# The first layer of three of eight experts as seven block products in place of eight, its stages set between second-layer tiles

## The chip, the cores and the metric

The kernel runs on one core of a Trainium2 chip. The time is that of the device from start to end of one execution, in microseconds. The engines are TensorE (PE, with PEld for its weight loads), VectorE (DVE), ScalarE (ACT), GpSimd (POOL) and SyncE (SP, which only issues DMAs here). Each works through a list of instructions of its own, in order, and waits for others by semaphores.

## The reference

A filter along the sequence in the frequency domain, then a mixture of eight experts, each of which takes exactly 2,496 tokens. Tokens are given out greedily by the sorted logits.

```python
def _attn_ref(x, filt_r, filt_i):              # x (8, 2496, 256)
    X = np.fft.rfft(x, axis=1)
    F = (filt_r + 1j * filt_i)[None, :, :]
    y = np.fft.irfft(X * F, n=x.shape[1], axis=1)

def _moe_ref(x, w_gate, w1, w2):               # x (19968, 256), E = 8
    cap = N // E
    logits = x @ w_gate
    order = np.argsort(-logits.flatten())
    ...
    for e in range(E):
        mask = assigned == e
        h = np.maximum(x[mask] @ w1[e], 0.0)   # 256 -> 1024
        out[mask] = h @ w2[e]                  # 1024 -> 256
```

## The kernel before

Up to 448 us the filter runs as matmuls with cosine tables. The logits `lg` are made beside it. From there to the end the eight experts e0 to e7 follow one another on PE, and this is the part that the change touches.

**One expert.** `Ffn.run` takes its tokens in five groups: four of 512 and one of 448. fp32 precision is kept by splitting each operand into a high part (rounded to fp32r, by ACT) and a low part (the rest, by DVE), and three products: high x high, high x low, low x high. `gather` brings tokens by indirect DMA, `turn` transposes them on PE (L837, four transposes for 256 tokens) and splits them (L840 on ACT, L841 on DVE). `first(g, f)` makes one of eight chunks of 128 hidden features for a group: two halves of the 256 inputs x three products, six matmuls of 512 (448) columns into one PSUM tile `pz` of four (L859). ACT writes the relu's high part (L865), DVE the low part (L873; L876 in the last group), for some chunks POOL (L868, L869). The second layer goes by tiles of 128 tokens: for each of the eight chunks a matmul of 512 columns (L913, the high part by both halves of the weights) and one of 256 (L914). ACT copies the result (L923), POOL adds its halves (L924) and scatters it (L925). The last tile has 64 tokens and takes 16 matmuls of 256 columns (L909). The weights of an expert are loaded whole (L804, on POOL) and split in pieces of 512 columns (L816 on ACT, L817 on DVE).

**What sets the order.** On PE the program's order holds. In group g the first layer of group g+1 is laid between the second-layer tiles of g (`firsts(g + 1, ORD[t])`). The lists of DVE, ACT and POOL come from a scheduler at build time and are fixed then.

**The routing.** While experts run, the next expert's tokens are chosen: `threshold` searches a limit by counting matmuls (L567, L580) with DVE work between them (L559, L577, L597 to L619), then come exact selection, a correction of the logits by `pen` (L696 on DVE, eight operations L727 on ACT) and the places of the tokens (L756 to L773). Each `yield c` of the expert's program passes c microseconds to `Pump.feed`, whose clock decides between which matmuls the next routing step stands. The routing of phase 7, the last, runs beside e5.

Of the kernel before, what the change touches and what calls it, by code (L numbers as in the profile page):

```python
# [27 lines left out]
NP, NZ, MZ, NXO, ZB, NH = 5, 4, 8, 4, 2, 10  # L28
# [441 lines left out]
class Route:  # L470
# [10 lines left out]
    def setup(s):  # L481
# [35 lines left out]
        s.tmp = t("tmp", [117, S, 8])  # L517
        s.iota, s.sidx = t("iota", [117, 512], F16), t("sidx", [128, 20])
        io = s.tmp.rearrange("p s e -> p (s e)")[:, :512]
# [117 lines left out]
    def phase(s, ph):  # L637
# [23 lines left out]
        vc, need, tot, mem = v("vc", [128, 1]), v("need", [128, 1]), v("tot", [117, 4]), v("m0", [117, S])  # L661
# [7 lines left out]
        if ph < 7:  # L669
# [15 lines left out]
            ga, eqm, cum = v("ga", [117, S]), v("eqm", [117, S]), v("cum", [117, S])  # L685
# [42 lines left out]
        with s.tc.issue_after(s.last):  # L728
            t, t3 = v("u", [117, S]), v("u2", [117, S])
# [54 lines left out]
class Ffn:  # L784


    def __init__(s, tc, i, xs, out, cp, ww, zp, ps):
# [6 lines left out]
        s.wt, s.xg, s.xT = {}, {}, {}  # L794

    def weights(s, e, widx):
# [3 lines left out]
        hl = [[s.ww.tile([128, 2048], F32R, name=f"w0{h}", bufs=2) for h in 'hl']]  # L800
        s.w2b = s.ww.tile([128, 2, 2048], F32R, name="w1", bufs=2)
        hl.append([s.w2b[:, k] for k in range(2)])
        s.wt[e] = (raw, hl, s.w2b)
        s.load = lambda k: nc.gpsimd.indirect_dma_start(out=raw[k], out_offset=None, in_=(s.w1, s.w2)[k], in_offset=off).ins  # L804

    def split(s, e, part):

        nc = s.nc
        raw, hl, _ = s.wt[e]
        k, h = divmod(part, 4)  # L810
        src, (hi, lo) = raw[k], hl[k]
        if k == 0:
            h, j = divmod(h, 2)
            h += 2 * j
        src, hi, lo = (t[:, 512*h:512*h+512] for t in (src, hi, lo))
        nc.scalar.copy(hi, src)  # L816
        nc.vector.tensor_tensor(lo, src, hi.bitcast(F32), op=OP.subtract)  # L817

    def gather(s, e, g, ids):
        for t in range(4*g, 4*g + 4):  # L820
            n = min(128, CAP - 128*t)
            xg = s.xg[e, t] = s.wp.tile([128, D], F32, name="xg", bufs=8)
            s.lastg = s.nc.gpsimd.indirect_dma_start(out=xg[:n], out_offset=None, in_=s.xs,  # L823
# [18 lines left out]

    def run(s, e, pump, hook):

        nc = s.nc
        ids = pump.out[e]
        out_rows = s.out
        _, ((w1h, w1l), (w2h, w2l)), w2 = s.wt[e]
        hs = {}

        def first(g, f):
# [4 lines left out]
            for k in range(2):  # L856
                sl = slice(1024*k+128*f, 1024*k+128*f+128)
                for w, x in ((w1h, xh), (w1h, xl), (w1l, xh)):
                    nc.tensor.matmul(p[:, :n], w[:, sl], x[:, k, :n], start=m == 0, stop=m == 5)  # L859
                    m += 1  # L860
                yield 0.65 * n / 512
# [283 lines left out]
```

## Time and profile before

| what | us |
|---|---|
| median of three runs | 1456.03 (1455.15 to 1462.08) |
| the profiled execution | 1465.58 |
| its span | 1463.8 |
| e5, e6, e7 begin | 1109.88, 1229.63, 1345.79 |
| last matmul ends | 1458.95 |
| PE busy | 1391.3 (95% of the span) |
| DVE, ACT, POOL busy | 955.6, 723.7, 663.6 |

The profiled execution lies above the median of the runs without a profile; all stretches below are its own. A matmul's record is longer than its distance to the next one, since matmuls overlap in the pipeline. So lengths of a stream are read from starts. A row of waits names the waiting instruction, then what released it.

### The profile page before, as it was taken

The numbers are of one execution on the slowest core, as the hardware profiler recorded it, in microseconds if no ns is written. First come the engines' busy times: TensorE is split into PE (matmuls) and PEld (weight loads), VectorE is DVE, ScalarE is ACT, GpSimd is POOL, SyncE is SP. The second block draws the span as 40 slices with busy tenths as digits, with TensorE's granted clock in tenths as the row PEclk, the third lists the DMA queues.
The fourth block names the chain that finished last, engine by engine and source line by source line (L and its number), as shares of the span: only waits on it lengthen the run. The fifth ranks groups of instructions, "written<-read, shape, count | busy, mean of one in ns | idle before, by whom it ended". The sixth has DMA issues, their size and how long they took to land. (4 is left out here: it accounts for less than half of the span.)

```text
span 1463.8 us, 24844 instructions
## 1 busy us (share of the span) xinstructions
PE 1391.3 (95%) x9127; PEld 1148.7 (78%) x9127; DVE 955.6 (65%) x2574; ACT 723.7 (49%) x1686; POOL 663.6 (45%) x729
## 2 busy tenths in 40 slices
PE   7899999998997999899999899999999999999998
PEld 6889899776445787677778788787878888888887
DVE  5666676576566789666876976977877854432231
ACT  5666677534473345344544533644553654533332
POOL 5433344243004745553664546366545644445423
PEclk9999999999998999999999999999999999999999
DMA  8554454888892102112110211211211221111100
GB/s 263 185 148 143 126 163 116 237 239 206 328 348 74 51 22 95 53 35 75 59 52 25 98 49 39 90 51 48 95 37 50 102 95 52 38 48 46 42 26 27
DMA packets 54780, 149.17 MB, mean 102 GB/s; under 512 B 9258, under 2 KB 29866, under 8 KB 50706
## 3 DMA queue, kind: packets, MB, share of 16 engines
q0 software_dynamic: 17552, 57.72, 12.1%
q1 hardware_dynamic: 9803, 47.11, 10.6%
q10 hardware_dynamic: 27304, 42.76, 9.5%
q8 instruction: 72, 1.18, 0.3%
q14 instruction: 49, 0.40, 0.1%
HBM read 83.89 MB, written 63.70 MB: 101 GB/s over the span
## 5 line engine op out<-in xcount | busy, mean ns | idle before, releaser
L913 PE MATMUL py<-w,hl 128*128 128x512 f32 x1216 | 445.6, 405 | 0.5 <-ACT hl L865 0.3
L914 PE MATMUL py<-w,hl 128*128 128x256 f32 x1216 | 341.9, 281 | 1.0 <-DVE hl L873 0.6
L865 ACT ACTIVATE hl<-pz 128x512 fp32r<-128x512 f32 (+1 forms) x320 | 186.8, 586 | 214.7 <-PE pz L859 189.0
L859 PE MATMUL pz<-xo,w0h 128*128 128x512 f32 (+1 forms) x640 | 264.4, 413 | 10.3 <-DVE hl L876 3.7
L913 PEld LDWEIGHTS py<-w,hl 128*128 128x128 f32 x1216 | 229.8, 189 | 51.4 <-issue 1.2
L924 POOL TENSOR_TENSOR y<-y 128x256 f32<-128x256 f32 x152 | 122.4, 806 | 311.2 <-ACT y L923 309.9
L859 PE MATMUL pz<-xo,w0l 128*128 128x512 f32 (+1 forms) x640 | 249.9, 390 | 0.0
L859 PE MATMUL pz<-z,w0h 128*128 128x512 f32 (+1 forms) x640 | 249.3, 390 | 0.2 <-issue 0.2
L914 PEld LDWEIGHTS py<-w,hl 128*128 128x128 f32 x1216 | 230.7, 190 | 5.3 <-DVE hl L873 2.2
L873 DVE SCALAR_TENSOR_TENSOR hl<-pz,hl 128x512 fp32r<-128x512 f32 x227 | 155.0, 687 | 116.0 <-ACT hl L865 101.8
L823 POOL DMA_INDIRECT xg<-xs,xid x160 | 168.3, 1052 | 135.8 <-issue 41.0
L923 ACT COPY y<-py 128x512 f32<-128x512 f32 x152 | 89.1, 586 | 282.8 <-PE py L914 188.5
L925 POOL DMA_INDIRECT out<-y,oid x160 | 174.5, 1090 | 48.1 <-POOL y L924 33.6
L859 PEld LDWEIGHTS pz<-xo,w0h 128*128 128x128 f32 x640 | 122.0, 191 | 33.7 <-DVE hl L873 3.8
L232 POOL TENSOR_TENSOR P<-P 128x256 f32<-128x256 f32 x80 | 58.9, 737 | 184.6 <-DVE P L230 184.5
L859 PEld LDWEIGHTS pz<-xo,w0l 128*128 128x128 f32 x640 | 121.3, 190 | 24.1
L859 PEld LDWEIGHTS pz<-z,w0h 128*128 128x128 f32 x640 | 122.0, 191 | 17.3 <-DVE z L841 1.0
L216 ACT COPY Y<-p 64x240 f32<-64x240 f32 (+1 forms) x304 | 116.0, 382 | 30.4 <-PE p L209 19.8
L209 PE MATMUL p<-cS,xr 117*128 117x120 f32 x688 | 100.5, 283 | 7.2 <-DMA xr<-xl 7.1
L559 DVE TENSOR_TENSOR Gm<-M,thr 117x1232 bf16<-117x1232 f32 (+2 forms) x80 | 105.5, 1329 | 0.2
L209 PEld LDWEIGHTS p<-cS,xr 117*128 117x128 f32 x688 | 91.0, 199 | 11.2 <-issue 4.7
L224 PE MATMUL p<-cW,Y 128*128 128x128 f32 x640 | 88.7, 281 | 2.3 <-ACT Y L216 1.5
(229 smaller groups left out, 2274.2 us busy)
## 6 DMA issues: line engine op xcount, KB each, us to landing
zd<-zt ACTq DMA_DIRECT2D x80, 256.0 KB
z<-zd SPq DMA_DIRECT2D x18, 600.0 KB
xs<-xo ACTq DMA_DIRECT2D x18, 600.0 KB
xr<-xl SPq DMA_DIRECT2D x6, 1404.0 KB
xr<-xl SPq DMA_DIRECT2D x7, 1111.5 KB
xr<-zd SPq DMA_DIRECT2D x8, 600.0 KB
xs<-xr ACTq DMA_DIRECT2D x8, 600.0 KB
xs<-Y ACTq DMA_DIRECT2D x6, 600.0 KB
```

Of the source, the lines that this page charges most:

```text
L209: nc.tensor.matmul(p[:, q-q0, :120], s.xr[b][:, q], s.cS1, start=True, stop=True)
L216: x = (nc.vector.tensor_copy if dve else nc.scalar.copy)(dst, src)
L559: nc.vector.tensor_tensor(Gm[:, s0:s1, :m], s.M[:, s0:s1].unsqueeze(2).to_broadcast([117, s1 - s0, m]), thr[:117].unsqueeze(1).to_broadcas ...
L823: s.lastg = s.nc.gpsimd.indirect_dma_start(out=xg[:n], out_offset=None, in_=s.xs, in_offset=bass.IndirectOffsetOnAxis(ap=ids[0][:n, t:t+1] ...
L859: nc.tensor.matmul(p[:, :n], w[:, sl], x[:, k, :n], start=m == 0, stop=m == 5)
L865: s.lasta = nc.scalar.activation(h[:, :n], p[:, :n], AF.Relu).ins
L873: nc.vector.scalar_tensor_tensor(l[:, :n], p[:, :n], 0.0, h[:, :n].bitcast(F32), op0=OP.max, op1=OP.subtract)
L913: nc.tensor.matmul(pp, hs[g][f][:, hi], w2[:, :, 256*f:256*f+256], start=f == 0, stop=False, skip_group_check=True)
L914: nc.tensor.matmul(pp[:, f % 2], hs[g][f][:, lo], w2h[:, 256*f:256*f+256], start=False, stop=f > 5, skip_group_check=True)
L923: s.lasta = nc.scalar.copy(yy, pp).ins
L924: nc.gpsimd.tensor_tensor(y, y, yy[:, 1], op=OP.add)
L925: st = nc.gpsimd.indirect_dma_start(out=out_rows, out_offset=bass.IndirectOffsetOnAxis(ap=ids[1][:w, 4*g+t:4*g+t+1], axis=0), in_=y[:w], i ...
```

## The change

For e5, e6 and e7 (`E0 = 5`) `run7` takes the place of `run`. The first layer of a group is cut in two halves of inputs (k), tokens and features, and computed by seven block products with sums of blocks of weights and of tokens, for eight (the Winograd form of Strassen's algorithm). A `step` makes 256 of 512 features of both halves for 512 tokens, 42 matmuls of 256 columns, in four stages: A (two products into `p11` and `pm`), B (two), C (two), D (one). Between them ACT copies `p11` to `pu` and `pm` to `m5`, DVE adds `p12 = pu + m5` and `c22 = pu + m5`, and C and D go on adding into `p12` and `pu`. `sums` makes the weights' sums (one on DVE, three on POOL) and splits seven pieces for four, `turns` the tokens' sums (three copies on ACT, four subtractions of 256 on DVE) and splits seven blocks. The second layer of a group is held back as a generator (`s.pend`) and laid in pieces of four matmuls, two after each stage of the next group's steps. The second layer of e4's last group goes into the first step of e5, and eight matmuls on constants stand at that border. Elsewhere: the second layer's pieces yield 0.7 for 0.65, in all experts; first-layer weights live in eight blocks of both parts; hidden tiles are 5 + 6 in two tags for 10; for e5 and on the routing's limit is raised at the second group.

```diff
+    def sums(s, e):
...
+        s.nc.vector.tensor_tensor(s1, r21, r22, op=OP.add)
+        tt(r21, r21, r11, op=OP.subtract)
...
+        s.xT[e, g] = dict(b11=u1[:, :, :256], b21=u1[:, :, 256:], t1=u2[:, :, :256], t2=u2[:, :, 256:],
+                          b22=u4[:, :, :256], t3=u3[:, :, :256], t4=u3[:, :, 256:])
...
+        def prods(*list):
+            for p, wk, xk, start in list:
+                for h in range(2):
+                    f = slice(128*(2*d+h), 128*(2*d+h)+128)
+                    for m, (i, j) in enumerate(((0, 0), (0, 1), (1, 0))):
+                        nc.tensor.matmul(p[:, 256*h:256*h+256], w[wk][:, i, f], x[xk][:, j],
+                                         start=start and h == m == 0, stop=m == 2, skip_group_check=True)
...
+        p11, pm = bank(), bank()
+        prods((p11, '11', 'b11', True), (pm, 's1', 't1', True))
+        pu = bank()
+        nc.scalar.copy(pu, p11)
+        m5, c22 = (s.wp.tile([128, 512], F32, name="hr", bufs=2) for _ in range(2))
+        nc.scalar.copy(m5, pm)
+        yield 1.42
+        prods((pu, 's2', 't2', False), (p11, '12', 'b21', False))
+        p12 = bank()
+        nc.vector.tensor_tensor(p12, pu, m5, op=OP.add)
+        relu(p11, 0, 0)
+        yield 1.42
+        prods((pu, 's3', 't3', False), (p12, 's4', 'b22', False))
+        nc.vector.tensor_tensor(c22, pu, m5, op=OP.add)
+        yield 1.42
+        relu(p12, 1, 0)
+        relu(c22, 1, 1)
+        prods((pu, '22', 't4', False))
+        relu(pu, 0, 1)
+        yield 0.71
...
+        lead = 4 if e == E0 else 0
+        for g in range(5):
...
+            for d in range(2):
+                for k, c in enumerate(s.step(e, g, d, H)):
+                    yield c
+                    for _ in range(4 if lead and d == 0 and k < 2 else 2):
+                        c = next(s.pend, None)
+                        if c:
+                            yield c
```

**PE's list, the end of e5's first group.** Before, a chunk of the next group (`pz_13810`, tokens `xo_13724`) stands behind three other chunks (those of `pz_13768`, `pz_13778`, `pz_13788`), and second-layer matmuls follow it:

```order
L859 MATMUL pz_13788<-xo_13376,w0h_12364 128x512 [waits DVE_49]
L859 MATMUL pz_13788<-z_13377,w0h_12364 128x512
L859 MATMUL pz_13788<-xo_13376,w0l_12365 128x512
L859 MATMUL pz_13788<-xo_13376,w0h_12364 128x512
L859 MATMUL pz_13788<-z_13377,w0h_12364 128x512
L859 MATMUL pz_13788<-xo_13376,w0l_12365 128x512
L707 LDWEIGHTS tri_3655
L707 MATMUL rt_13795<-tb_13684,tri_3655 117x2 [waits DVE_49]
L859 MATMUL pz_13810<-xo_13724,w0h_12364 128x512 [waits Activation_49]
L859 MATMUL pz_13810<-z_13725,w0h_12364 128x512
L859 MATMUL pz_13810<-xo_13724,w0l_12365 128x512
L859 MATMUL pz_13810<-xo_13724,w0h_12364 128x512
```

After, at the same place (line numbers are those of the changed kernel, L919 its first layer), the second step of group 0: C into `pu` (`pz_13627`) and `pz_13653`, D into `pz_13627`, then stage A of group 1, `pz_13713` and `pz_13714`:

```order
L886 MATMUL ptr_13658<-id_4814,xg_13335 128x128
L919 MATMUL pz_13627<-z_13305,w0_13308 128x256 [waits DVE_49]
L919 MATMUL pz_13627<-z_13305,w0_13308 128x256 x5
L919 MATMUL pz_13653<-xo_13298,w0_13311 128x256 x6
L919 MATMUL pz_13627<-z_13305,w0_13314 128x256 [waits DVE_49]
L919 MATMUL pz_13627<-z_13305,w0_13314 128x256 x5
L919 MATMUL pz_13713<-z_13638,w0_13170 128x256 [waits PE_49,Activation_49]
L919 MATMUL pz_13713<-z_13638,w0_13170 128x256 x5
L919 MATMUL pz_13714<-xo_13666,w0_13173 128x256 [waits PE_49,Activation_49]
L919 MATMUL pz_13714<-xo_13666,w0_13173 128x256 [waits DVE_49]
L919 MATMUL pz_13714<-xo_13666,w0_13173 128x256 x4
```

No second-layer matmuls stand between these stages; D waits for DVE, A's second product for ACT and DVE.

**ACT's list at that place.** Before, the logits' correction (L727) stands between relus of two chunks:

```order
L865 ACTIVATE hl_13750<-pz_13743 128x512 [waits DVE_49,PE_49]
L840 CAST xo_13724<-ptr_13753 128x2x256 [waits PE_49]
L865 ACTIVATE hl_13775<-pz_13768 128x512 [waits DVE_49,PE_49]
L865 ACTIVATE hl_13785<-pz_13778 128x512 [waits DVE_49,PE_49]
L727 ACTIVATE lg_69<-lg_69,pen_13716 117x176 [waits DVE_49]
L727 ACTIVATE lg_69<-lg_69,pen_13716 117x176 x7
L865 ACTIVATE hl_13807<-pz_13788 128x512 [waits PE_49,Activation_49]
L865 ACTIVATE hl_13817<-pz_13810 128x512 [waits PE_49,Activation_49]
L923 COPY y_13858<-py_13820 128x512 [waits DMASW5_49,PE_49,Pool_49]
```

After, it (L729) stands ahead of the step's last two relus (L926) and of the high part of the tokens' sums `xo_13666`, which stage A of group 1 reads; L933 is the next step's copy of `p11`:

```order
L894 COPY tmp_3685<-ptr_13658 128x256 [waits PE_49]
L926 ACTIVATE hb_13698<-pz_13653 128x512 [waits DVE_49,PE_49]
L812 CAST z_13667<-ptr_13658 128x256 [waits DVE_49]
L729 ACTIVATE lg_69<-lg_69,pen_13599 117x176 [waits DVE_49]
L729 ACTIVATE lg_69<-lg_69,pen_13599 117x176 x7
L926 ACTIVATE hb_13701<-hr_13630 128x512 [waits DVE_49]
L926 ACTIVATE ha_13710<-pz_13627 128x512 [waits PE_49]
L812 CAST xo_13666<-tmp_3685 128x512 [waits DVE_49,Activation_49]
L812 CAST xo_13695<-tmp_3685 128x512 [waits DVE_49]
L933 COPY pz_13727<-pz_13713 128x512 [waits PE_49]
```

What stood ahead of two chunks' relus stands ahead of two relus and a token operand.

**DVE's list at that place.** Before, between the low parts (L873) of chunks:

```order
L873 SCALAR_TENSOR_TENSOR hl_13750<-pz_13743,hl_13750 128x512 [waits Activation_49]
L841 TENSOR_TENSOR z_13725<-ptr_13753,xo_13724 128x2x256 [waits Activation_49]
L691 CAST tb_13684<-tot_13682 117x2 [waits DVE_49]
L666 TENSOR_SCALAR ev_13686<-val_3680,vc_13680 128x8
L694 SCALAR_TENSOR_TENSOR cum_13705<-one_3670,eqm_13704 117x176
L873 SCALAR_TENSOR_TENSOR hl_13775<-pz_13768,hl_13775 128x512 [waits Activation_49]
L667 SCALAR_TENSOR_TENSOR ej_13687,eid_13688<-ev_13686,row_3652 128x8 [waits DVE_49]
L696 TENSOR_SCALAR pen_13716<-ev_13686 128x8
L668 SCALAR_TENSOR_TENSOR widx_13689<-eid_13688,row_3652 128x1 [waits DVE_49]
L873 SCALAR_TENSOR_TENSOR hl_13785<-pz_13778,hl_13785 128x512 [waits Activation_49]
```

After, from the sum `p12` (L939) to the sum `c22` (L943), with the routing's L693 to L698, token low parts (L813) and token sums (L895, L896) between them:

```order
L939 TENSOR_TENSOR pz_13653<-pz_13627,hr_13629 128x512 [waits PE_49,Activation_49]
L703 MEMSET tot_13965 117x4
L813 TENSOR_TENSOR z_13638<-ptr_13632,z_13638 128x512 [waits Activation_49]
L693 CAST tb_13567<-tot_13565 117x2 [waits DVE_49]
L668 TENSOR_SCALAR ev_13569<-val_3680,vc_13563 128x8
L696 SCALAR_TENSOR_TENSOR cum_13588<-one_3670,eqm_13587 117x176
L928 SCALAR_TENSOR_TENSOR ha_13655<-pz_13613,ha_13655 128x512 [waits Activation_49]
L895 TENSOR_TENSOR tmp_3685<-ptr_13658,tmp_3685 128x256 [waits Activation_49]
L896 TENSOR_TENSOR tmp_3685<-ptr_13658,tmp_3685 128x256
L669 SCALAR_TENSOR_TENSOR ej_13570,eid_13571<-ev_13569,row_3652 128x8 [waits DVE_49]
L698 TENSOR_SCALAR pen_13599<-ev_13569 128x8
L943 TENSOR_TENSOR hr_13630<-pz_13627,hr_13629 128x512 [waits PE_49]
```

The two sums that stages C and D wait for stand in one row with the routing and the splits.

## Rows read from the trace of the kernel before

**Rows 1.** Waits of PE, 448 to 1459 us: us in total, times, longest.

```profile
PE rt L567 <- DVE ex L769: 7.3, 4, 2.7
```

**Rows 2.** Waits of PE in e5, 1109.88 to 1229.63 us, all.

```profile
PE py L914 <- DVE hl L873: 0.2, 1, 0.2
```

**Rows 3.** e5 to e7: length, busy PE, PEld, DVE, ACT, POOL, then PEclk, DMA.

```profile
1109.88:1229.63 119.75, 119.27 (x686) 99.24 (x685) 75.48 (x247) 57.78 (x128) 60.79 (x66) 1.00 0.24 79
1229.63:1345.79 116.16, 116.14 (x622) 98.04 (x621) 46.94 (x122) 52.03 (x117) 53.12 (x60) 1.00 0.14 45
1345.79:1458.95 113.16, 113.16 (x594) 96.53 (x592) 32.70 (x57) 38.72 (x68) 43.54 (x51) 1.00 0.11 35
```

**Rows 4.** Timeline of PE, first layer, 512 and 448 columns: start, us, instruction.

```profile
586.57 0.40 PE L859 MATMUL pz<-z,w0h 128*128 128x512 f32 x1
586.80 0.39 PE L859 MATMUL pz<-xo,w0l 128*128 128x512 f32 x1
...
1333.84 0.37 PE L859 MATMUL pz<-xo,w0l 128*128 128x448 f32 x1
1334.05 0.37 PE L859 MATMUL pz<-xo,w0h 128*128 128x448 f32 x1
```

**Rows 5.** PE's timeline at a half tile; the page's weight loads of L913.

```profile
583.61 2.11 PE L909 MATMUL py<-w,hl 128*128 128x256 f32 x16
...
585.09 0.63 PE L909 MATMUL py<-w,hl 128*128 128x256 f32 x4
...
L913 PEld LDWEIGHTS py<-w,hl 128*128 128x128 f32 x1216 | 229.8, 189 | 51.4 <-issue 1.2
```

**Rows 6.** Timeline of PE, the filter's 256-column matmuls with full weights.

```profile
78.37 0.28 PE L279 MATMUL pa<-yh,cEl 128*128 128x256 f32 x1
78.49 0.28 PE L279 MATMUL pa<-yh,cEh 128*128 128x256 f32 x1
```

**Rows 7.** Timeline of DVE: 512-wide operations one behind another, e5.

```profile
1116.19 0.68 DVE L873 SCALAR_TENSOR_TENSOR hl<-pz,hl 128x512 fp32r<-128x512 f32 x1
1116.80 0.68 DVE L841 TENSOR_TENSOR z<-ptr,xo 128x512 fp32r<-128x512 f32 x1
```

**Rows 8.** Busy time of DVE in the first 60 us of e5.

```profile
1109.88:1130.00 20.12, 15.57 (x39) 1.00 0.19 57
1130.00:1150.00 20.00, 14.97 (x59) 1.00 0.21 58
1150.00:1170.00 20.00, 16.43 (x58) 1.00 0.36 137
```

**Rows 9.** DVE's operations by form, 1109.88 to 1170: busy, mean ns.

```profile
L559 DVE TENSOR_TENSOR Gm<-M,thr 117x1232 bf16<-117x1232 f32 x3 | 4.3, 1443 | 0.0
L758 DVE SCALAR_TENSOR_TENSOR OH<-iota,BC,oa 117x512 f16<-117x512 f16 x3 | 2.6, 876 | 0.0
L619 DVE TENSOR_REDUCE di<-o 128x1 int32<-128x7 int32 x5 | 0.8, 159 | 0.1
L689 DVE SCALAR_TENSOR_TENSOR eqm<-eqm,vc,one 117x176 f32<-117x176 f32 x1 | 0.4, 400 | 0.0
```

**Rows 10.** Timeline of ACT: 512-wide operations one behind another.

```profile
1242.46 0.60 ACT L865 ACTIVATE hl<-pz 128x512 fp32r<-128x512 f32 x1 [0.40 <-PE pz L859]
1242.95 0.61 ACT L816 CAST w0h<-wr 128x512 fp32r<-128x512 f32 x1
```

**Rows 11.** Source line L727 in e5: ns min/median/max, first and last start.

```profile
L727 ACT ACTIVATE lg<-lg,pen x8: 622/642/681, 1147.0 to 1150.8; 117x176 f32<-117x176 f32 x8
```

**Rows 12.** Timeline of PE behind a long idle time in e1.

```profile
591.31 0.18 PE L580 MATMUL rt<-X,ones 128*128 128x18 f16 x1 [2.75 <-DVE X L577]
```

**Rows 13.** Busy time and granted clock of PE behind it.

```profile
592.40:595.80 3.40, 3.40 (x13) 0.51 0.36 96
```

**Rows 14.** Source lines L804 (weight load) and L816 (its first use) in e5.

```profile
L804 POOL DMA_INDIRECT wr<-w1l,widx x1: 947/947/947, 1147.4 to 1147.4; - x1
...
L816 ACT CAST w0h<-wr x3: 618/623/624, 1153.6 to 1161.4; 128x512 fp32r<-128x512 f32 x3
```

More of the change, by code (lines that the diff above doesn't have):

```diff
@@ new lines, in second @@
+    def second(s, e, g, t, H, order):
+        nc, ids, w2 = s.nc, s.pids[e], s.wt[e][2]
+        w = min(128, CAP - 512*g - 128*t)
+        half = w == 64
+        pp = s.ps.tile([128, 2, D], F32, name="py", tag="b", bufs=2)
+        p = pp[:, 0]
+        for m, f in enumerate(order):
+            hi, lo, both = H(t, f)
+            w2h, w2l = (w2[:, k, 256*f:256*f+256] for k in range(2))
+            if half:
+                nc.tensor.matmul(p, both, w2h, start=m == 0, stop=False, skip_group_check=True)
+                nc.tensor.matmul(p[:64], hi[:, :64], w2l, start=False, stop=m == 7, skip_group_check=True)
+            else:
+                nc.tensor.matmul(pp, hi, w2[:, :, 256*f:256*f+256], start=m == 0, stop=False, skip_group_check=True)
+                nc.tensor.matmul(pp[:, m % 2], lo, w2h, start=False, stop=m > 5, skip_group_check=True)
+            if m in (1, 3, 5):
+                yield 0.45 if half else 0.7
+        yy = s.wp.tile([128, 2, D], F32, name="y", bufs=4)
+        y = yy[:, 0]
+        if half:
+            nc.scalar.copy(y[:w], p[w:])
+            nc.vector.tensor_tensor(y[:w], p[:w], y[:w], op=OP.add)
+        else:
+            s.lasta = nc.scalar.copy(yy, pp).ins
+            nc.gpsimd.tensor_tensor(y, y, yy[:, 1], op=OP.add)
+        st = nc.gpsimd.indirect_dma_start(
+            out=s.out, out_offset=bass.IndirectOffsetOnAxis(ap=ids[1][:w, 4*g+t:4*g+t+1], axis=0),
+            in_=y[:w], in_offset=None)
+        for o in s.scat:
+            s.tc.declare_no_dep(st.ins, o.ins, reason="each token has one place")
+        s.scat.append(st)
+        yield 0.45 if half else 0.7
@@ L843, in run, with seconds @@
+    def seconds(s, e, g, H, order):
+        for t in range(4):
+            yield from s.second(e, g, t, H, order)
     def run(s, e, pump, hook):
         nc = s.nc
-        ids = pump.out[e]
-        out_rows = s.out
-        _, ((w1h, w1l), (w2h, w2l)), w2 = s.wt[e]
+        blk = s.wt[e][1]
         hs = {}
@@ L995, in weights @@
                 R.wdma = W.load(1)
-            split.extend((e, p) for p in range(8))
+            split.extend((e, p) for p in range(0 if e < E0 else 4, 8))
         pump.on_w = weights
@@ L1043, in hook @@
                         flush(8)
+                    elif what == 'limit':
+                        pump.limit = e + 1
                     elif isinstance(what, tuple):
```

208 lines of the change are left out of this document (149 added, 59 removed).

## The prediction, made before the changed kernel ran

> **What bounds the kernel now.** I read the waits of PE first, over all eight experts: the largest entry, 7.3 us in four times, is a counting matmul of the routing that waits for DVE [rows 1]. Then the same view for the sixth expert (e5), where the change begins: 0.2 us in 120 [rows 2]. The busy time by expert says the same of all three changed experts: PE is busy 119.27 of 119.75, 116.14 of 116.16 and 113.16 of 113.16 us, with DVE at 75.48, 46.94 and 32.70 us and ACT and POOL at about half or less [rows 3]. So in these 349 us the number and length of PE's matmuls set the time, and a shorter list is worth its full length only as long as PE stays fed. What feeds it is fastest to lose in e5, where the last routing phase still runs on DVE: 15.57 of 20.12, 14.97 of 20 and 16.43 of 20 us busy in its first 60 us [rows 8].
>
> **PE's list.** Removed: per expert 4 groups x 8 chunks x 6 = 192 matmuls of 512 columns and 48 of 448. One to the next takes 0.23 and 0.21 us (586.57 to 586.80; 1333.84 to 1334.05) [rows 4]; over longer runs of the same rows I take 0.2285 and 0.205. Three experts: 3 x (192 x 0.2285 + 48 x 0.205) = 161.1 us. Added: 10 steps of 42 matmuls of 256 columns, 1,260 in all. The 448-column last group gets padded, which this count holds. Their pitch is the one price that no row shows for this line, so I bound it. The last four of a half tile's 16 matmuls of 256 columns take 0.63 us from 585.09 [rows 5]; less the last one's own 0.28 that is three pitches of 0.117, but every second weight there is 64 columns wide. The filter's 256-column matmuls with full weights follow each other by 0.12 and are 0.28 long [rows 6]. I take 0.1175: 1,260 x 0.1175 = 148.0 us, between 147.0 and 151.2. Eight matmuls at the border of e4 and e5 that only set flags (four of 512 columns) cost 4 x 0.23 and a little, 1.0. Second layer, transposes and the routing's matmuls keep their number. Sum for PE: 148.0 + 1.0 - 161.1 = **-12.1 us** (-13.1 to -8.9).
>
> **What the steps add on ACT, DVE and POOL.** Each step has four stages A to D with two handovers that PE did not have before: the sum p12 on DVE between B and the second half of C, and the reading of pu on DVE (c22) between C and D, besides the copy of p11 on ACT between A and B. A 512-wide operation follows the last by about 0.6 on DVE (0.68 long) [rows 7] and 0.49 on ACT (0.60 long) [rows 10]. Copies from PSUM to PSUM and sums into PSUM have no row; I price them like the nearest (PSUM to SBUF, 0.60 and 0.68), with half as much again as the upper end. In a step with its cover, PE has between two stages four second-layer pairs, 4 x (0.23 + 0.117) = 1.4 us, and another product of 0.7 us. 2.1 us hide 0.6 to 0.7 of work with its queue. So for e6, e7 and the later groups of e5 the handovers cost nothing; each that loses its cover costs 0.7 and what stands ahead in the queue. In a group of these experts (22 us) ACT has some 19 of such operations (10 us), DVE as much. POOL gets three 512-wide subtractions per expert; it was busy 61 of 120 us at most [rows 3]. At the borders e5 to e6 and e6 to e7 the weights' sums are made in one piece from the raw weights, whose load stands on POOL behind the gathers: a load issued at 1147.4 was first used at 1153.6 [rows 14], so the first split can come late by part of those 6 us. I take 0.5 for both borders, 0 to 3.
>
> **The opening of e5** is where the cover is missing. The held-back second layer of e4's last group is used up within the first step, so the second step of group 0 has no second-layer pieces in it: PE has 1.4 us per stage and eight transposes, and needs DVE twice and ACT twice. And DVE's list there still holds the routing. I counted its list from one p12 sum to the next, over the first four steps: 34, 37, 28 and 44 instructions. In them are 35 of 512 columns (at 0.60 us 21.0), 10 of 256 (half of that and a little, 3.4), one count matrix and its short piece (1.44 for the long one, 2.0 together), 9 place selections (0.88 for the longest form, overlapping; 4.0), 17 of 176 columns (up to 0.40, overlapping; 5.3) and 70 small ones (0.16 long, overlapping; 8.8): 44.4 us [rows 7, 9]. By step that is 10.4, 11.9, 9.1 and 13.0, against 12.9, 5.8, 10.7 and 11.8 us of PE work. The second step stands out: 11.9 of DVE in 5.8 of PE, and DVE can't work it ahead, since its entries follow that step's products.
>
> Followed through the queues: p12 comes 0.8 us late, behind the routing's entries. The c22 sum stands behind 2.8 us of entries that follow p12 (a token lo-part, a hidden lo-part, two token sums, the routing's rows), while PE has 1.4 us in C, and a handover: D starts 2.1 late. Ahead of c22 stands `pen`, which releases eight operations on ACT that correct the logits. They run in one piece, from 1147.0 to 1150.8 plus the last one's 0.64, 4.4 us [rows 11]. Before, they hurt nothing: PE had four PSUM tiles and second-layer work, and no wait is seen [rows 2]. Now the two relus of the step and the token sum's hi-part, which the next group's second product reads, stand behind them; counted from `pen`, ACT needs 4.4 + 3 x 0.49 and DVE another 0.8 for the lo-part, 6.7 us, and PE has c22's 0.7, D and the first product, 2.1. That gives 4.6 us idle. After it 0.5 in the next step. At the start of group 2 the token sum's lo-part stands behind a hidden lo-part and the routing's entries: 2.5. At the border of e4 and e5 the routing's wait for X comes with less work around it: 0.8. Sum **11.3**, between 5 (the logits' block alone, with a little) and 16 (these sums at the upper prices and at the busy share that DVE reached before).
>
> **Clock.** After PE had idled 2.75 us before 591.31, the granted clock was 0.51, the 1.2 GHz level, from 592.4 to 595.8 [rows 12, 13]: 3.4 us at half rate, 1.7 lost. Other idle pieces of about 2 us had no such stretch behind them. Of the idle pieces above one of 4.6 and two of 2 to 2.5 qualify; I take one loss, 1.7 (0 to 5.1).
>
> **Experts 0 to 4** keep their matmuls. The second layer's pieces now count 0.7 instead of 0.65 to the clock that deals out the routing, so its rounds come some 4% sooner. The waits at one of its two counting matmuls are 7.3 us in all now [rows 1]. A round that is closer to its answer can wait longer, one that ends sooner frees the border: I take 0, from -4 to +2.
>
> **Sum** against the profiled execution of 1465.6 us: -12.1 + 11.3 + 0.5 + 1.7 - 0.2 (e5's old wait) = +1.2. That execution lies 9.5 above the median of 1456.0; no term depends on that, so I carry the difference over: **1457.2**. Half a percent, about what can be told from no change, is 7.3 us: faster is under 1448.7, slower over 1463.3.
>
> **Rivals.** *The opening is short (faster).* If DVE works through the routing's entries before the second step, only the logits' block is left: 4.5. -12.1 + 4.5 - 0.2 = -7.8 gives 1448.2, and less with a gain in experts 0 to 4. For it: the routing's rows are placed by a scheduler that had the same wait in view, and DVE was never over 0.82 busy in that time [rows 8]. Against: 11.9 against 5.8 in one step. Chance 0.24.
>
> *DVE becomes the bound of four steps (slower).* If DVE reaches only the 0.78 that it had on average in e5's first 60 us (46.97 of 60.12) [rows 8], the four steps take 44.4 / 0.78 = 56.9 in place of 41.2: 15.7. With 0.8 at the border, 0.5 at the later ones and three stretches of half clock (5.1): -12.1 + 15.7 + 0.8 + 0.5 + 5.1 - 0.2 = +9.8, 1465.8. It decides from 19.1 us of opening and clock together. Against: a queue that is the bound runs closer than one that waits. Chance 0.20.
>
> *Weights don't hide behind 256 columns (slower by far).* There are 540 more weight loads, 0.189 us each [rows 5]. If none ran beside a matmul, they would add 540 x 0.189 = 102 us to the sum above, 1559. Against it: a half tile's 16 matmuls with their 16 loads took 2.11 us, where 16 loads in line with 16 matmuls would need over 4 [rows 5]. What is left is a pitch that is a little longer, 0.127, the load's row not hidden in full: 1,260 x 0.0095 = 12 more, 1469. Chance 0.02 for both. The Trainium skill, "TensorE: Matmul & The Clock Gate", section "The mechanism", says that a load overlaps matmuls in flight only when the row group differs; all loads here fill the whole array, so this rival is what its rule would give, and the trace disagrees with it, by the 2.11 us.
>
> **How the numbers follow.** Forecast (no change) 0.54, short opening 0.24, DVE bound 0.20, weights 0.02. So faster 0.24, same 0.54, slower 0.22. Range: low end with opening 5, no clock loss and 4 gained in the first experts, -11.3: 1444. High end with opening 16, clock 3.4, borders 3 and 2 lost in the first experts, +12: 1468. That holds most of both neighbours; about 0.18 is outside.
>
> **What would show it.** In the new profile the first-layer matmuls of the seven products should follow by 0.115 to 0.12; e6 and e7 should take about 4 us less each with no wait of PE over a microsecond. In e5 PE should idle 8 to 13 us, most of it in its first 50 us, once for over 4 us behind the logits' operations on ACT, and before that about 2 behind c22; DVE should be over 0.85 busy there. A granted clock of 0.5 should follow once. Wrong: a pitch over 0.125; waits in every step; an e5 that is shorter than before by 3 us or more; experts 0 to 4 that differ by more than 4 us together.

## The result, and the profile after

The changed kernel takes 1468.32 us (median of 19 runs, 1460.35 to 1474.76) against 1456.82 us (19 runs, 1449.42 to 1471.42). The ratio is 1.0069, interval 1.0046 to 1.0091: 0.7% slower, some 10 us (the two medians lie 11.5 us apart). The forecast was no change, 1457; the median lies 0.3 us past the range of 1444 to 1468, the ratio times the 1456.03 that the prediction had, 1466.1, inside it.

The two profiled executions show only 4.4 us of it (1469.97 against 1465.58 us), because that of before lies 9 us above its median and that of after 1.7. A second profile of before (the first experiment below) shows where these 9 us were. The table gives the length of each expert, from its first first-layer matmul to the next one's, worked out from the starts in the traces; "filter" is the start of e0.

| | filter | e0 | e1 | e2 | e3 | e4 | e5 | e6 | e7 |
|---|---|---|---|---|---|---|---|---|---|
| before, the profile of the prediction | 448.2 | 138.0 | 138.7 | 131.3 | 127.6 | 126.1 | 119.8 | 116.2 | 113.2 |
| before, again | 446.6 | 136.9 | 131.3 | 130.9 | 127.5 | 126.1 | 119.8 | 116.2 | 113.2 |
| after | 446.9 | 139.2 | 134.0 | 132.5 | 128.5 | 125.4 | 120.6 | 115.2 | 121.2 |
| after without the seven products (E0 = 8) | 448.2 | 138.8 | 134.1 | 132.5 | 128.4 | 128.8 | 118.9 | 116.3 | 113.6 |

From e2 on the stages of before repeat within half a microsecond, while the filter, e0 and e1 do not. So the comparison is made from e2 to the end: 743.3 us after, 734.0 and 733.6 before, **+9.5 us**, close to the 10 us of the ratio. One shift has to be taken into account: the second layer of an expert's last group now runs behind the next expert's first matmul. That is three tiles of 8 x 0.3475 (a pair of matmuls, 0.23 + 0.1175) and a half tile of 16 x 0.117, 10.2 us, at each border; at that of e4 and e5 one tile of 2.8 stands ahead of the new start, so that only 7.4 move. On equal terms e4 to e7 after are 132.8, 123.4, 115.2 and 111.0 us.

Busy time by engine, after, e4 to e7 (columns as in [rows 3], which these lines answer to):

```profile
980.99:1106.39 125.40, 119.56 (x735) 95.51 (x731) 103.50 (x309) 61.49 (x138) 68.17 (x66) 0.99 0.18 59
1106.39:1227.01 120.62, 113.73 (x814) 104.62 (x813) 90.50 (x266) 75.61 (x167) 62.48 (x63) 0.97 0.21 69
1227.01:1342.22 115.21, 111.97 (x803) 103.65 (x801) 76.58 (x173) 72.40 (x161) 61.70 (x64) 1.00 0.17 55
1342.22:1463.38 121.16, 119.31 (x838) 110.88 (x836) 58.99 (x107) 59.30 (x109) 49.53 (x57) 1.00 0.10 35
```

PE, which was busy nearly all the time in e5 to e7 [rows 3], now idles 6.9 us in e5, 3.2 in e6 and 1.9 in e7, and DVE carries 90.5, 76.6 and 59.0 us for 75.5, 46.9 and 32.7. What PE waits for in e5's first 54 us, where it waited 0.2 in the whole expert [rows 2]:

```profile
PE pz L919 <- ACT xo L812: 3.6, 1, 3.6
PE pz L919 <- DVE hr L943: 1.5, 1, 1.5
PE rt L766 <- DVE xo L813: 1.0, 1, 1.0
PE pz L919 <- DVE xo L813: 0.4, 1, 0.4
```

The first two are the two waits of the prediction's second step. PE's timeline (start, length, instruction, idle time before it and its releaser) shows them one behind the other: D behind c22, then A of group 1 behind the high and the low part of the tokens' sums.

```profile
1126.93 1.68 PE L919 MATMUL pz<-z,w 128*128 128x256 f32 x12 [1.55 <-DVE hr L943]
...
1132.23 0.58 PE L919 MATMUL pz<-xo,w 128*128 128x256 f32 x1 [3.62 <-ACT xo L812]
...
1133.16 1.44 PE L919 MATMUL pz<-xo,w 128*128 128x256 f32 x5 [0.35 <-DVE xo L813]
```

ACT's timeline there, the logits' block of [rows 11] ahead of two relus and the tokens' sums:

```profile
1126.42 4.25 ACT L729 ACTIVATE lg<-lg,pen 117x176 f32<-117x176 f32 x8
1130.56 0.63 ACT L926 ACTIVATE hb<-hr 128x512 fp32r<-128x512 f32 x1
1131.08 0.59 ACT L926 ACTIVATE ha<-pz 128x512 fp32r<-128x512 f32 x1
1131.55 1.14 ACT L812 CAST xo<-tmp 128x512 fp32r<-128x512 f32 x2
```

DVE's timeline there, with what stood ahead of c22 (L943), and its own idle time behind the block:

```profile
1123.57 0.68 DVE L813 TENSOR_TENSOR z<-ptr,z 128x512 fp32r<-128x512 f32 x1
...
1124.36 0.52 DVE L696 TENSOR_TENSOR_SCAN cum<-one,eqm 117x176 f32<-117x176 f32 x1
1124.80 0.66 DVE L928 SCALAR_TENSOR_TENSOR ha<-pz,ha 128x512 fp32r<-128x512 f32 x1
1125.38 0.41 DVE L895 TENSOR_TENSOR tmp<-ptr,tmp 128x256 f32<-128x256 f32 x1
...
1126.12 0.16 DVE L698 TENSOR_SCALAR pen<-ev 128x8 f32<-128x8 f32 x1
1126.20 0.68 DVE L943 TENSOR_TENSOR hr<-pz,hr 128x512 f32<-128x512 f32 x1
...
1131.22 0.69 DVE L928 SCALAR_TENSOR_TENSOR hb<-hr,hb 128x512 fp32r<-128x512 f32 x1 [2.68 <-ACT hb L926]
```

`pen` (L698) ends at 1126.28; the eight operations on the logits hold ACT from 1126.42 to 1130.67, and the tokens' sums follow at 1131.55. PE had nothing else, and DVE itself stood idle for 2.68 us: this wait is ACT's. Behind it the granted clock was at its 1.2 GHz level, as it had been in e1 [rows 13]; busy time and clock of PE there:

```profile
1132.20:1138.00 5.80, 5.42 (x20) 0.52 0.63 254
```

At their usual distances these matmuls would have taken 2.2 us less.

**The price of a product.** PE's timeline in a step of e6, a product of six matmuls. It takes 0.87 us, the last one's own 0.28 included, so 0.118 from one to the next. Over all 1,260 the mean distance, waits left out, is 0.1186, where the prediction took 0.1175 from [rows 5, 6].

```profile
1248.01 0.87 PE L919 MATMUL pz<-z,w 128*128 128x256 f32 x6
```

**The starts of e6 and e7.** Here the prediction saw almost nothing, and each costs 1.4 us, with 0.7 more at the second group's stage A (both counted as matmul distance above the usual). DVE's timeline at the start of e6:

```profile
1222.08 1.40 DVE L813 TENSOR_TENSOR w<-wr,w 128x512 fp32r<-128x512 f32 x1
...
1225.01 2.40 DVE L813 TENSOR_TENSOR w<-wr,w 128x512 fp32r<-128x512 f32 x2
1227.33 0.41 DVE L813 TENSOR_TENSOR xo<-ptr,xo 128x256 fp32r<-128x256 f32 x1
1227.66 0.41 DVE L901 TENSOR_TENSOR tmp<-tmp 128x256 f32<-128x256 f32 x1
...
1228.53 0.67 DVE L813 TENSOR_TENSOR z<-tmp,z 128x512 fp32r<-128x512 f32 x1
```

PE's timeline there:

```profile
1229.26 0.86 PE L919 MATMUL pz<-z,w 128*128 128x256 f32 x5 [1.26 <-DVE z L813]
```

The token sums' low part (z, 1228.53) waits for the sum L901, which stands behind low parts of the weights (w, L813). The one at 1222.08 takes 1.40, the pair behind it 2.40, where one takes 0.68 elsewhere. e7 shows the same rows; by distance the two waits are 1.42 and 1.43 us.

**e4.** The longest single wait from e0 on stands in an expert whose matmuls the change leaves alone. A one-hot row of the routing (OH, L760) takes 4.07 us on DVE, where L758, the same operation, took 0.88 on average in e5 before [rows 9]; POOL runs two sums of e5's weights (L832, L835) and a hidden low part (L1013) in that time; and PE waits for X (L579), which stands behind it on DVE. DVE's timeline:

```profile
1042.60 4.07 DVE L760 SCALAR_TENSOR_TENSOR OH<-iota,BC,oa 117x512 f16<-117x512 f16 x1
...
1048.96 0.15 DVE L579 TENSOR_TENSOR X<-D,row 48x6 f16<-48x6 f32 x1
```

POOL's timeline in the same stretch:

```profile
1042.34 1.30 POOL L832 TENSOR_TENSOR wr<-wr 128x512 f32<-128x512 f32 x1
1043.59 1.29 POOL L1013 TENSOR_TENSOR hb<-hr,hb 128x512 fp32r<-128x512 f32 x1
1044.83 1.27 POOL L835 TENSOR_TENSOR wr<-tmp,wr 128x512 f32<-128x512 f32 x1
```

PE's timeline, the matmul ahead of the wait and the one behind it:

```profile
1044.89 0.40 PE L1003 MATMUL pz<-xo,w 128*128 128x512 f32 x1
1049.16 0.19 PE L582 MATMUL rt<-X,ones 128*128 128x6 f16 x1 [3.87 <-DVE X L579]
```

Busy time and clock of PE behind it:

```profile
1049.00:1052.40 3.40, 3.24 (x10) 0.51 0.00 0
```

3.87 us idle, and 3.4 us at half clock behind it, 1.7 more. How much of this the held row makes, the experiment on the weights' sums shows below. And not all of it counts against the kernel without the seven products: in its e4 that one waits 2.24 us for a hidden low part, with a stretch at half clock behind it too.

### The profile page after: what moved, and what is told of

The parts are those of the page before. It is cut to its first block, busy times and chain, and to the rows that moved or that the text cites. A ratio compares the mean times of both kernels' runs of the same rounds, so it can differ in the third digit from the quotient of the medians.

```text
span 1468.2 us, 26251 instructions
## 1 busy us (share of the span) xinstructions
PE 1385.4 (94%) x9675; PEld 1167.7 (80%) x9675; DVE 1038.7 (71%) x2727; ACT 785.9 (54%) x1812; POOL 678.6 (46%) x738
## 5 line engine op out<-in xcount | busy, mean ns | idle before, releaser
L1003 PE MATMUL pz<-xo,w 128*128 128x512 f32 (+1 forms) x800 | 283.2, 406 | 6.2 <-DVE hb L1020 1.9
L976 POOL TENSOR_TENSOR y<-y 128x256 f32<-128x256 f32 x152 | 128.5, 846 | 307.9 <-ACT y L975 306.5
L965 PE MATMUL py<-w,ha 128*128 128x512 f32 x620 | 249.4, 415 | 1.4 <-ACT y L975 1.4
L965 PE MATMUL py<-w,hb 128*128 128x512 f32 x596 | 231.0, 400 | 0.5 <-ACT hb L1009 0.5
L852 POOL DMA_INDIRECT xg<-xs,xid x160 | 169.6, 1060 | 111.0 <-issue 26.0
L1003 PEld LDWEIGHTS pz<-xo,w 128*128 128x128 f32 x800 | 152.5, 191 | 38.2 <-DVE ha L1017 3.5
L966 PE MATMUL py<-w,ha 128*128 128x256 f32 x620 | 175.0, 282 | 0.0
L966 PE MATMUL py<-w,hb 128*128 128x256 f32 x596 | 168.4, 282 | 1.3 <-DVE hb L1017 1.2
L1003 PE MATMUL pz<-z,w 128*128 128x512 f32 (+1 forms) x400 | 156.8, 392 | 0.4 <-DVE z L870 0.4
L965 PEld LDWEIGHTS py<-w,ha 128*128 128x128 f32 x620 | 118.8, 192 | 23.7 <-ACT y L975 1.8
L965 PEld LDWEIGHTS py<-w,hb 128*128 128x128 f32 x596 | 112.8, 189 | 25.5 <-ACT hb L1009 1.1
L966 PEld LDWEIGHTS py<-w,ha 128*128 128x128 f32 x620 | 119.2, 192 | 1.4
L966 PEld LDWEIGHTS py<-w,hb 128*128 128x128 f32 x596 | 113.3, 190 | 2.6 <-DVE hb L1017 2.1
L919 PE MATMUL pz<-z,w 128*128 128x256 f32 x756 | 109.9, 284 | 4.4 <-DVE z L813 2.8
L919 PEld LDWEIGHTS pz<-z,w 128*128 128x128 f32 x756 | 97.0, 188 | 7.8 <-DVE z L813 3.7
```

Of the source, the lines that this page charges most:

```text
L919: nc.tensor.matmul(p[:, 256*h:256*h+256], w[wk][:, i, f], x[xk][:, j], start=start and h == m == 0, stop=m == 2, skip_group_check=True)
L965: nc.tensor.matmul(pp, hi, w2[:, :, 256*f:256*f+256], start=m == 0, stop=False, skip_group_check=True)
L966: nc.tensor.matmul(pp[:, m % 2], lo, w2h, start=False, stop=m > 5, skip_group_check=True)
L976: nc.gpsimd.tensor_tensor(y, y, yy[:, 1], op=OP.add)
L1003: nc.tensor.matmul(p[:, :n], w1[:, i], x[:, k, :n], start=m == 0, stop=m == 5)
```

## The experiments

Two theories stood against each other. "Opening and borders": what the seven products earn is lost at the places just shown. "Rhythm": the loss lies in e0 to e4, by the routing rounds that come sooner (yields of 0.7). All kernels start from the changed one but the first, which is before itself; each diff is against the changed kernel or against the experiment named ahead of it.

**Before, once more.**

> The kernel before, once more, for a second profile. The profiled execution that the prediction rests on lies 9 us above its median. Theory 'unlucky profile': this one ends e0 to e4 some 5 to 10 us sooner than the first (661.6 us from e0's first matmul to e5's), with fewer of the waits of 2 to 3 us at the counting matmuls and fewer half-clock stretches; e5 to e7 stay at 349 us within 1. Rival: the first profile is typical and the profiler itself costs the difference: e0 to e4 within 2 us of 661.6.

1455.1 us. e0 to e4 took 652.7 us for 661.6, e5 to e7 the same 349.1. The first profile had been unlucky in e0 and e1 by 8.5 us. The theory holds, and with it goes the prediction's "no term depends on that": the stretch that differs is one that the change touches, so single profiles of e0 and e1 say nothing about it. The filter's part, whose lists are the same in all these kernels, ended between 441 and 460 us in the 14 profiles. A scatter of that size there would cover a large part of the some 20 us among the runs of one kernel.

**Without the seven products, and with the old yields.**

```diff
-E0 = 5
+E0 = 8
...
-            last = g == 4 and e + 1 == E0
+            last = g == 4 and e + 1 == E0 < 8
```

> The changed kernel without its seven products: E0 = 8, so all experts use the old first layer, but the blocks of weights, the two tags of hidden tiles, the single routing buffers and the yields of 0.7 stay. 'Opening and borders': no difference to before, a ratio of 0.998 to 1.002. 'Rhythm': slower by 4 to 8 us, 1.003 to 1.005.

1465.35 us (12 runs), ratio 1.0047, interval 1.0013 to 1.0081. By the middle of the intervals, which overlap with that of the changed kernel, two thirds of the loss remain without a single product of seven.

```diff
-                yield 0.45 if half else 0.7
+                yield 0.325 if half else 0.65
...
-        yield 0.45 if half else 0.7
+        yield 0.325 if half else 0.65
```

> E0 = 8 as in the second experiment, and besides the yields of before (0.65). What is left of the change are the weights' blocks, the hidden tiles' two tags and the single routing buffers. If the sooner routing rounds cost the 7 us of the second experiment, this one is back at before: a ratio of 0.998 to 1.002. If the buffers cost them: 1.003 to 1.006.

1463.1 us (12 runs), ratio 1.0022, 0.9995 to 1.0049: between the two expected values. By stage it is clearer: e2 to e4 take 390.0 us, 389.7 with yields of 0.7, and 384.5 and 384.9 in before. The size of the yields is not what these 5 us hang on. But PE's list of before did not come back with it: the rewritten second layer yields four times in its half tile, where before yielded twice, and from e0's half tile on the routing's matmuls stand elsewhere (e2 holds 780 matmuls, 795 with yields of 0.7, 769 in before).

> The changed kernel with one part undone: the second layer's pieces yield 0.65 again (the half tile's four 0.325) in place of 0.7 (0.45), so the routing's clock runs as before; everything else stays. Theory 'opening and borders' (the loss lies in e5's opening and in the starts of e6 and e7): the time stays within 2 us of the changed kernel, a ratio to before of 1.006 to 1.009. Rival 'rhythm' (the loss lies in e0 to e4, whose routing rounds come sooner): 4 to 8 us less, a ratio of 1.001 to 1.004.

1479.85 us (6 runs), ratio 1.0129, 1.0088 to 1.0169. Neither theory had this. e5 takes 127.3 us for 120.6: with the slower clock more of the last phase stands in e5's opening, and new waits appear there (2.43 us of a routing matmul behind the token sums' low part on DVE, 2.16 of the transposes). In e5's first 50 us stand 74 of the routing's matmuls for 33, and the logits' block runs only behind them; PE's wait for the low part of the tokens' sums on DVE is 1.97 us here without that block. So the yield of 0.7 is no cost of the change: with 0.65 e2 to e4 take 386.1 us for 386.3, and e5 takes 6.7 more.

**Which of the remains.** Both kernels are that without the seven products and with the old yields, with buffers put back; the expectations here call it the sixth experiment, and the one that comes first here the ninth.

> The kernel of the sixth experiment (no seven products, yields of 0.65) with the hidden tiles as one tag of ten and the routing's tiles double again, one look. Of the change only the weights' blocks and the shared scratch tile stay. The stages e2 to e4 repeat within 1 us between profiles of before (384.5 and 385.0 in sum) and took 387.7 to 390.0 in the kernels with the new buffers. If hidden tiles or routing tiles cost that: 384 to 386. If the blocks or the scratch do, or the order that the scheduler finds: 388 or more.

> As the ninth, but the hidden tiles stay in two tags, of five each; only the routing's tiles are double again. If single routing tiles cost the 3 to 5 us of e2 to e4: 384 to 386 in sum; if the two tags do: 387 or more while the ninth is under 386.

388.5 and 387.4 us for e2 to e4. Both stay well above 385, and the one that restores more buffers is the longer one. By the expectation that leaves the weights' blocks, the shared scratch or the order that the scheduler finds for DVE, ACT and POOL; and a fourth that it does not name, PE's own list. In both kernels the lists of PE, DVE, ACT and POOL in e0 to e4 are those of the kernel without the products and with the old yields, operation by operation, with the routing's matmuls where that has them and not where before has them. So putting buffers back took 1.5 to 2.6 us off e2 to e4 without moving an operation in these lists; for the other 3 us no run shows the cause, and single profiles differ by 1 us. It stays open which it is.

**The logits' block.**

```diff
-        for e in range(8):
+        for e in range(8 if ph < 6 else 0):
             nc.scalar.activation(s.lg[:, :, e], ...
```

> The changed kernel without the last of the logits' corrections (eight operations on ACT at the end of phase 6; phase 7 reads no logits, so the output stays). If that block makes the 3.8 us wait of A of e5's second group, the wait falls under 1 us, no half-clock stretch follows (1.3 us), and the time falls by 3 to 5 us, a ratio to before of 1.003 to 1.005. If DVE's low part is late anyway: 1 us or less.

1471.2 us (12 runs), ratio 1.0087, 1.0056 to 1.0118: no gain that can be measured. In the profile the block's wait shrinks as expected, from 3.62 to 0.49 us and 0.91 for the low part, and no stretch at half clock follows. But new waits stand behind it, for p12 and c22. PE's timeline of this kernel, the rows with a wait:

```profile
1127.42 1.69 PE L919 MATMUL pz<-z,w 128*128 128x256 f32 x12 [1.55 <-DVE hr L943]
...
1129.60 0.38 PE L919 MATMUL pz<-xo,w 128*128 128x256 f32 x1 [0.49 <-ACT xo L812]
...
1130.89 0.85 PE L919 MATMUL pz<-xo,w 128*128 128x256 f32 x5 [0.91 <-DVE xo L813]
...
1137.77 0.95 PE L919 MATMUL pz<-xo,w 128*128 128x256 f32 x6 [1.68 <-DVE pz L939]
...
1141.27 0.97 PE L919 MATMUL pz<-xo,w 128*128 128x256 f32 x6 [0.42 <-DVE hr L943]
```

e5 takes 118.3 us for 120.6. So the block was the cause of that wait, as the prediction has it, and DVE's list was next: of 6.8 us (3.8 and 0.8 of wait, 2.2 of clock) 2.3 came back.

**The cover spread over both steps.**

```diff
-        lead = 4 if e == E0 else 0
+        lead = 0
```

> The changed kernel with the held-back second layer of e4 spread over both steps of e5's first group (two pieces behind each stage, none ahead of the first), as in all later groups. If the missing cover in the second step makes the waits of 1.7 (D behind c22) and 3.8 us (A of group 1 behind the logits' operations), both shrink by 1.4 us of second-layer work per stage: PE idles 3 to 6 us less there. Against it the first step loses its lead, so that its A may wait for the tokens' and weights' sums by up to 3 us. Net -3 us, from -6 to +1. If the waits come from the length of DVE's list alone, the waits only move: 0.

1474.42 us (8 runs), ratio 1.0096, 1.0057 to 1.0136. The waits moved and did not shrink: the wait for c22 is gone, A of the second group waits 2.3 (0.37 and 1.97) for 4.0, but the first step now waits 0.96 and 0.34 for its tokens' sums, C 0.82 for a hidden tile, and a routing matmul 2.05 for DVE. Its waits of PE from 1100 to 1166:

```profile
PE rt L766 <- DVE xo L813: 2.1, 1, 2.1
PE pz L919 <- DVE xo L813: 2.0, 1, 2.0
PE pz L919 <- ACT z L812: 1.0, 1, 1.0
PE pz L919 <- DVE ha L928: 0.8, 1, 0.8
```

e4 and e5 together, which hold the same matmuls in both kernels, take 248.1 us here for 246.0; part of that is a second stretch at half clock, behind the routing matmul. That speaks for the length of DVE's list as the bound of the opening, with the missing cover deciding only where it shows.

**Two experts for three.**

```diff
-E0 = 5
+E0 = 6
```

> The seven products in e6 and e7 only (E0 = 6), with the yields of before (0.65). PE's list is 8.4 us shorter, not 13.1. If e5's cost is that the routing's last phase stands in DVE's and ACT's lists beside a step without cover, e6's opening costs under 4 us here and the start of e7 2.3: the last two experts together take 1 to 3 us less than before's, and the time lies at 0.998 to 1.002 of before if the old rhythm is without cost. If the opening costs some 10 us wherever it stands: 1.004 or more.

1466.49 us (12 runs), ratio 1.0049, 1.0017 to 1.0081. From e5 on the experts take 350.9 us, 1.8 more than in before, but not because e6 and e7 earn nothing. With the second layer's shift at the borders taken into account (7.4 and 10.2 us, as above) they take 115.2 and 110.9 us for 116.2 and 113.2: 3.3 less, a little more than the 1 to 3 expected. e6's opening stands without the threshold rounds and costs 0.8 (c22) and 1.0 (tokens), the routing's last places 1.4, e7's start 1.3. The loss is in e5, 124.8 on the same terms for 119.8: the border's eight matmuls, some 1.0, and one wait for a hidden low part ahead of the transposes with a stretch at half clock behind it. PE's timeline there:

```profile
1161.81 1.11 PE L866 MATMUL ptr<-id,xg 128*128 128x128 f32 x4 [2.71 <-DVE ha L1017]
```

DVE's timeline there, and POOL's:

```profile
1156.54 1.98 DVE L813 TENSOR_TENSOR w<-wr,w 128x512 fp32r<-128x512 f32 x1
...
1161.07 0.68 DVE L1017 SCALAR_TENSOR_TENSOR ha<-pz,ha 128x512 fp32r<-128x512 f32 x1
```

```profile
1155.96 1.31 POOL L839 TENSOR_TENSOR wr<-wr 128x512 f32<-128x512 f32 x1
1157.22 0.74 POOL L976 TENSOR_TENSOR y<-y 128x256 f32<-128x256 f32 x1
```

Between 45 and 60 us into e5 DVE makes one of e6's weights' sums and eight low parts of weights, three of them stretched to 2.88, 1.80 and 1.98 us beside POOL's sums; without the products (old yields) the weights' low parts lie between 45 and 72 us and PE has no such wait. So here what the two experts earn is lost in the expert ahead of them, which makes their weights while the routing still runs.

**The weights' sums.**

```diff
-        tt = s.nc.gpsimd.tensor_tensor
+        tt = s.nc.vector.tensor_tensor
```

> The changed kernel with the three subtractions of the weights' sums on DVE in place of POOL, one look. In its profile DVE's low parts of the weights took 1.0 us on average and up to 1.4 while a POOL operation ran, and 0.68 otherwise. If POOL's subtractions stretch them, those rows come back to 0.68 outside the second layer's additions on POOL, DVE's list at the border is about as long as before (three more at 0.6, two or three less stretched by 0.4 to 0.7), and the waits of 1.4 us at the starts of e6 and e7 stay between 0.8 and 2.0. If the stretch has another cause, the rows stay long and the waits grow by 1.8, to over 3 us.

One run, 1486.0 us, whose filter ended at 459.6; so only stages count. The OH row in e4 is back at 1.06 us, with one POOL operation beside it for three. DVE's timeline there:

```profile
1055.01 1.06 DVE L760 SCALAR_TENSOR_TENSOR OH<-iota,BC,oa 117x512 f16<-117x512 f16 x1
...
1056.60 0.68 DVE L835 TENSOR_TENSOR wr<-tmp,wr 128x512 f32<-128x512 f32 x1
```

POOL's timeline there:

```profile
1054.25 1.28 POOL L1013 TENSOR_TENSOR hb<-hr,hb 128x512 fp32r<-128x512 f32 x1
```

In the five kernels with yields of 0.7 that had the sums on POOL it took 4.07 or 4.08 us, and no other of the 40 rows took over 1.2. So POOL's sums did hold it. But the wait for X hardly shrinks, and a stretch at half clock follows as before. PE's timeline there:

```profile
1060.38 0.19 PE L582 MATMUL rt<-X,ones 128*128 128x6 f16 x1 [3.25 <-DVE X L579]
```

On DVE L832, L835 and two more low parts of the new weights now stand ahead of X and eat what the end of the hold gave: e4 is 1.0 us shorter. The waits at the starts of e6 and e7 rise from 1.4 to 2.5 and 2.7. That is between the two expectations: the stretch is part of those waits and not all of them. What is shown, then, is that the hold costs DVE some 3 us in e4, and that PE waits over 3 us there with the sums on either engine.

**Later sums.**

```diff
-                        if k < 3:
+                        if k in (0, 2):
                             next(s.todo)
+                    if d == 0 and g == 0 and e > E0 and k == 0:
+                        next(s.todo)
```

> The changed kernel with the weights' sums and splits for e6 and e7 later: the second piece (s2, 12) behind stage C instead of B of the last step, the third (s3, s4, 22) behind stage A of the new expert's first step. If the 1.4 us wait of PE at each of these starts is the token sums' low part queued behind the weights' low parts on DVE, it falls under 0.5 us at both, and e5 to e7 take 2 us less (357.0 us before that, in three kernels within 1). If the later pieces come too late, stages B to D of that step wait for them instead, 1 us or more in all.

Nothing changed: 1.40 and 1.42 us of wait, e5 to e7 357.6 us for 357.0. The reason is no answer to the question: DVE's list is the same as in the changed kernel but for buffer numbers (543 operations in e5 to e7, in the same order; so are those of PE, ACT and POOL). The scheduler sets the rows where it did, wherever the program writes them. So the queueing at the borders is read from the rows above and was not tested by a kernel in which the order differs.

**Both edits.**

> The changed kernel with both edits that take waits from e5 to e7: no last logits' correction and later sums. By their profiles, 2.3 us in e5 and 2 us at the borders: 1464, a ratio to before of 1.003 to 1.006. Faster than before (under 1.000) is not expected, as the first experts' 5 us and most of e5's opening stay.

1474.25 us (6 runs), ratio 1.0113, 1.0077 to 1.015. With the last experiment without effect this is the kernel without the logits' block once more: e5 118.5 us, e5 to e7 354.8 in both, though this profile has a stretch of 3.4 us at half clock in e5. That the two medians lie above the changed kernel's although e5 is 2 us shorter is not explained by the stages from e2 on; its filter ended at 457.9 in the profile. No version of this study beats before.

## Why the prediction came out as it did

It forecast no change; the kernel is 0.7% slower, just over the half percent, a case that had been given 0.22. The terms summed to +1.2 us, the stages give +9.5. By its own steps:

- **PE's list, -12.1.** 1,260 x 0.1186 for 148.0 is 1.4 more; with the eight matmuls at the border about -11. Within its bounds of -13.1 and -8.9. Weights hid behind 256 columns, as [rows 5] had it.
- **The opening, 11.3.** The gaps, as distance above the usual, are 1.7 (D behind c22; 2.1 predicted), 3.8 and 0.8 (A behind the logits' block and behind the low part; 4.6 for both), 1.6 at group 2 (2.5), 0.3 for p12 (0.8), 0.8 at the border (0.8): 9.0, some 9.3 with small ones. Mechanism, order and places were right. The longest of them is ACT's, not DVE's: DVE was idle for 2.68 us of it. That DVE's list would hold PE in its place, the second rival's claim, is what the experiments on the yields, the block and the cover speak for; it was not tested by a kernel with a shorter list on DVE. The four steps took 51.1 us, from the p12 sum at 1111.97 to that at 1163.03, between the 41.2 of PE's work and the 56.9 of that rival, so its price was too high. The claim that DVE would be over 0.85 busy was half right: 0.81, 0.76 and 0.91 in three windows of 20 us.
- **Clock, 1.7.** One stretch behind A's wait, as forecast, 2.2 lost. The step's reading that other idle pieces of about 2 us had no such stretch was wrong, and that the count came out was luck in part: in the profile of before those of 1.85, 1.76 and 2.42 us that ended at 571.2, 681.1 and 841.4 had one behind them, and that of 2.72 that ended at 600.9 had none.
- **The borders, 0.5 (0 to 3).** e6 and e7 were to have no wait over a microsecond; there are 1.4 at each start, 0.7 at each second group and 1.6 at a routing matmul in e6, some 5.9 in all. This step failed. It looked for the weights' load, which came in time, and not at what 7 splits for 4 and the token sums do to DVE's list in that one step, though it had counted just this list for the opening.
- **POOL's three subtractions, at nothing.** This failed too, and by the same cover that was named: POOL had time, but DVE did not while POOL ran. One row of e4 was held for 4.07 us in place of 0.75. The price was not POOL's alone, since with the sums on DVE PE waited 3.25 us at the same place. On equal terms e4 took 4.0 us more than without the seven products: 2.8 of longer waits (5.8 for 3.0; both kernels have one stretch at half clock there) and 1.0 of the border's matmuls, which the first term holds.
- **Experts 0 to 4, 0 (-4 to +2).** Without the seven products e2 to e4 are 5.0 us longer than in before. The step looked only at the yields' size; that is not it. Buffers, blocks, the half tile's four yields and the lists that follow from them had been given no price at all, and which of them it is stays open.

By stages, on equal terms, the sum closes: 5.0 in e2 to e4 and -0.3 behind them from what remains without the products; from the products 4.0 in e4, 4.5 in e5 (-4.1 of matmuls, the opening, the clock, less what e5 waited without them), -1.1 in e6 and -2.6 in e7. Together +9.5. What the sum of +1.2 missed is mainly the 5.0 of the first experts, the 4.0 of e4 and the waits of e6 and e7. Only e7, which has no routing beside it, comes near its 4 us.

## What to carry to other kernels

A shorter list on the engine that is the bound has to be paid for on the engines that feed it: count each of their lists from handover to handover, at every place where the new work bunches, borders as well as the opening, and not only where the routing stands. The expert ahead, which prepares the operands, is such a place. A cover named as "this engine has time" has to hold for the neighbour that shares something with it. And where a profiled execution is off its median, compare stages that repeat between two profiles before a difference is carried over.

## What the runs showed of the hardware

DVE's operations on SBUF can be held while POOL runs an operation on SBUF; in the changed kernel those with an input in PSUM were not. There the weights' low parts (both inputs in SBUF, 128 x 512) took 0.68 us on average in 58 cases without a POOL tensor operation beside them and 0.99, up to 1.40, in 15 with one, of which five took no more than 0.69. The hidden low parts (one input in PSUM) took 0.69 and 0.68. The OH row, also with both inputs in SBUF, was held for 4.07 us, past the boundaries of three POOL operations in a row. The Trainium skill has this as an exclusive lock ("SBUF — State Buffer", section "SBUF: two separate sides"): a DVE operation with two SBUF inputs and a GpSimd one that reads SBUF share a port pair, and who comes first holds it for the whole instruction. The OH row agrees, and adds that DVE was not let in between POOL's instructions. Who came first does not settle every case: a low part at 1225.01 took 1.26 us although POOL's record beside it starts only at 1225.60. Nor is the hold new with the change: in before a short row of the routing (L610, 0.16 us alone) took 1.87 beside a POOL operation.

Copies from PSUM to PSUM on ACT and sums into PSUM on DVE, which no row of before had shown, cost about as much as their neighbours that write SBUF. ACT's groups by line, after, 1106 to 1464 us (L935 writes SBUF, L933 PSUM; busy us, mean ns):

```profile
L935 ACT COPY hr<-pz 128x512 f32<-128x512 f32 x30 | 17.6, 588 | 5.3 <-PE pz L919 4.0
L933 ACT COPY pz<-pz 128x512 f32<-128x512 f32 x30 | 17.3, 578 | 2.0 <-PE pz L919 0.3
```

DVE's groups by form, after, 980 to 1464 us (L939 writes PSUM, L943 SBUF):

```profile
L939 DVE TENSOR_TENSOR pz<-pz,hr 128x512 f32<-128x512 f32 x30 | 21.0, 698 | 56.9 <-PE pz L919 53.3 <-issue 3.5
L943 DVE TENSOR_TENSOR hr<-pz,hr 128x512 f32<-128x512 f32 x30 | 20.6, 686 | 10.3 <-PE pz L919 10.2
```
